# One fused kernel (linear attention, dense units, eight experts): a hand-given order at the passage from the dense units to the experts

## The chip, the core and the metric

The kernel runs on one core of a Trainium2 chip. The metric is the device time in microseconds (us) of one execution, as the median of three runs. The core's engines run side by side, each through its own queue in order: PE (TensorE: matrix products, its weight loads shown as PEld), DVE (VectorE), ACT (ScalarE), POOL (GpSimd) and SP (which here only issues DMAs). They wait for each other through semaphores.

## The reference

Three stages stand one behind the other. A recurrent attention over 768 steps gives 1536 rows (tokens) of 320 numbers. A dense pair of layers follows, and then a top-1 mixture of experts:

```python
def _moe_ref(x, w_in, w_out):                  # 320 -> 2048 -> 320
    h = x @ w_in
    g = np.maximum(0.01 * h, h)
    return (g @ w_out).astype(np.float32)

def _moe2_ref(x, w_gate, w1, w2, capacity):    # 8 experts, capacity 384
    logits = x @ w_gate
    expert_idx = np.argmax(logits, axis=1)
...
    for i in range(N):                          # places in the order of the tokens
        e = expert_idx[i]
        if counts[e] < capacity:
            disp[e, counts[e]] = x[i]
...
    h = np.maximum(np.einsum('ecd,edf->ecf', disp, w1), 0.0)
    y = np.einsum('ecf,efd->ecd', h, w2)
```

The row that a kept token gets back is its gate weight times the row of `y` at its place.

## The kernel before

**Tiles.** The 1536 tokens are twelve tiles of 128, grouped for routing into four blocks: tiles 0 to 3, 4 to 7, 8 to 10 (block 2) and 11 alone (block 3). A value that a product needs in full precision is held as two f16 parts, a high and a low one, so that a product is made of three (or, in the first layers, eight) products of f16.

**Dense units.** `unit(tl, c0, ncc)` makes hidden chunks c0 to c0+ncc-1 (of 16) for the tiles `tl`: eight products per chunk into the PSUM tile `h` (two buffers), then on ACT `t`, on DVE `t` again (the maximum), on ACT the high part `gh`, on POOL the low part `gl`. Its second layer, `close_unit`, comes two units later (LAG is 2): three products per chunk and tile into `px`. When the sixteenth chunk of a tile is in, `route_rows` takes `px` to a row `x2r` (for tile 11 a row that is called `zero`): `split_rows` writes the high part on ACT (L435), the low part on DVE (L436), and copies 64 columns of both on POOL (L439, "the duplicate").

**Routing of a block.** `route_logits` turns the rows (`x2T`): for blocks 0 to 2 by a transposing DMA on SP (L617), for block 3 by six PE transposes into `pt` and one DVE copy (L622, L623). Then come the logits `plg` on PE, the one-hot choice of expert `roh` on DVE, and the products `pp` (L654), which count the tokens ahead of each. `route_scatter` makes of `pp` the place of every token (`slot`) and scatters the rows to the DRAM table `scr`, one indirect DMA on POOL per tile.

**The first expert's input.** Expert e reads its 384 rows by a transposing DMA from `scr` into `xe` (`exp_load`, L822), and `mt` holds the gate weights of all (L827). The first expert does not wait for the last scatters: `exp_first` reads what blocks 0 and 1 put there, and `merge_open` and `merge_close` add the rows of blocks 2 and 3 by products: for each of six parts `pm`, one product with `xe`, three with block 2's rows and the one-hot places `oh`, one with tile 11's. Six casts (three on ACT, L688, three on DVE, L690) bring the sums back.

**Experts.** For each expert, up to three tiles of 128 rows (the second and third under `tc.If`): `hidden` (64 products), `evict` (ACT `hh`, DVE `hl`), `outs` (24 products into `py`), `deliver` (ACT `ye` with `mt`, POOL scatter to the output). Weights come in pieces of 512 hidden columns: a dense `w_in` or `w1` part (`wa`) and a `w_out` or `w2` part (`wc`), each split into high and low parts by `w_in_split` and `w_out_split` on ACT and DVE (L497, L498); pieces 4 and 5 are the first expert's, 6 and 7 the second's. The staging tiles `wa` and `wc` have four buffers each in the expert stage. During an expert, `some(k)` puts a share of the next splits (`bg`) between its steps.

**What sets the order.** A table `ORDER` names the steps in program order: `u11:8+4` is a unit of tile 11, `so6` the `w_out` split of piece 6, `rl2` and `rs2` the two routing steps of block 2, `fl` closes all open units. Up to the end of this table the framework's scheduler is free to put each engine's instructions in another order by its own estimate. From `tc.manual_schedule` on (ahead of the loop over experts) PE, DVE and ACT run in program order; POOL and SP stay the scheduler's.

Of the kernel before, what the change touches and what calls it, by code (L numbers as in the profile page):

```python
# [9 lines left out]
F16 = mybir.dt.float16  # L10
BF16 = mybir.dt.bfloat16
I32 = mybir.dt.int32
# [6 lines left out]
P = 128  # L19
# [28 lines left out]
u2-3:8+2 dec8 x7 og9 u2-3:14+2 tr8 u2-3:0+2 kw7 ld9 st7 cast9 u4-7:7+1 sc8 u4-7:3+1 rl0 kw8 lam9 dec9 tr9 eg8  # L48
# [3 lines left out]
u8-10:3+1 u8-10:8+1 rl1 u8-10:1+1 og11 eg11 st11 u8-10:13+1 u8-10:0+1 dec11 wi5 si5 tr11 sc11 u8-10:7+1 av11  # L52
u8-10:10+1 zf0 wi6 wo4 so4 wo5 si6 out11 x11 sw u8-10:11+1 wl7 wl8 rs1 u8-10:6+1 u8-10:9+1 u8-10:12+1
u8-10:5+1 u8-10:4+1 u8-10:15+1 xe so5 wo6 si7 u11:8+4 so6 u11:4+4 wl9 rl2 so7 rs2 u11:12+4 u11:0+4 fl rl3 rs3
# [3 lines left out]
def program():  # L58
    p = []
    for w in ORDER.split():  # L60
        if w[0] == "u":
            tl, c, n = w[1:].replace("+", ":").split(":")
            tl = [int(x) for x in tl.split("-")]
            p.append(("u", list(range(tl[0], tl[-1] + 1)), int(c), int(n)))
# [10 lines left out]
def tile_mlstm_moe_moe(  # L75
# [358 lines left out]
    def split_rows(r, src, scale, eng):  # L434
# [161 lines left out]
    def route_rows(i, px):  # L596
        bi, o = block_of[i]
        n = len(blocks[bi])
        if bi not in R:
            if n == 1:  # L600
                xr = zero.unsqueeze(1)
            else:
                xr = rows.tile([P, 4, ROW], F32, tag="x2r", name=f"x2r{bi}")
                nc.gpsimd.memset(xr[:, 0:n, 386:], 0.0)
            nc.gpsimd.tensor_scalar(out=xr[:, 0:n, 384:385], in0=tokid[:, i - o:i - o + n].unsqueeze(2), scalar1=1.0,
                                    scalar2=1.0, op0=ALU.mult, op1=ALU.mult)
            R[bi] = xr, a1.tile([P, 4, 6, P], F16, tag="x2T", name=f"x2T{bi}")
        split_rows(R[bi][0][:, o].bitcast(F16), px, 1.0 / (S_IN * S_OUT * S_G), nc.vector)

    def route_logits(bi):  # L610
# [3 lines left out]
        for o in range(n):  # L614
            xo = xr[:, o].bitcast(F16)[:, 0:6 * P]
            if bi < len(blocks) - 1:
                nc.sync.dma_start_transpose(out=x2T[:, o], in_=xo)  # L617
            else:
# [22 lines left out]
        def over_o(x):  # L641
            return x.unsqueeze(1).to_broadcast([P, n, E])
# [6 lines left out]
        nc.vector.tensor_tensor(out=oh, in0=over_o(dec), in1=over_e(u[1]), op=ALU.is_equal)  # L649

# [5 lines left out]
        nc.vector.reciprocal(u[2], inv_all[:, i0:i0 + n])  # L656
        nc.vector.scalar_tensor_tensor(out=t[3], in0=t[1], scalar=1.0 / S_WG, in1=over_e(u[2]), op0=ALU.mult, op1=ALU.mult)
        nc.scalar.activation(t[3], t[3], AF.Exp)
# [33 lines left out]
    def route_scatter(bi):  # L692
# [8 lines left out]
        nc.vector.tensor_tensor(out=base, in0=pp[:, n], in1=base, op=ALU.add)  # L701
# [63 lines left out]
    def unit(tl, c0, ncc):  # L765
# [18 lines left out]
        if len(open_units) > LAG:  # L784
            close_unit()

    def close_all():
        while open_units:
            close_unit()
# [9 lines left out]

    def w_load(n):  # L800
        w_alloc(n)
        w_load_in(n)
        w_load_out(n)
# [3 lines left out]
            "wi": w_load_in, "wo": w_load_out, "si": w_in_split, "so": w_out_split, "u": unit, "fl": close_all,  # L807
            "rl": route_logits, "rs": route_scatter, "zf": zero_fill, "gw": gate_weights}
# [31 lines left out]
    ENG = mybir.EngineType  # L840
    MINE = {ENG.PE, ENG.DVE, ENG.Activation}
# [45 lines left out]
    one = ExitStack()  # L887
    one.enter_context(tc.manual_schedule(engines=MINE))
    for n in range(4, E * NP2):
        pool_of[NP1 + n] = wpb if n % NPC < 3 else pool_of[NP1 + 3] if n % NPC == 3 else wpc  # L890
    for e in range(E):
# [4 lines left out]
        bg = []  # L896
# [82 lines left out]
```

## Time and profile before

| what | value |
|---|---|
| three timed runs | 432.55, 431.89, 428.73 us; median 431.89 |
| the profiled execution's own time | 429.85 us |
| its span from the first to the last instruction | 428.1 us (mean granted TensorE clock 0.965 of full) |
| PE busy | 368.8 us (86%) |
| DVE busy | 296.7 us (69%) |
| ACT busy | 231.3 us (54%) |
| POOL busy | 186.1 us (43%) |

The time is the span and 1.75 us around it. A busy share is a mean over stages: the dense units end near 296 us, the routing of the last tiles lies between 289 and 309 us, and the experts take the rest. Durations and positions in this document are of this one execution.

### The profile page before, as it was taken

Reading aid. Unit: us, or ns where it says so; the run is one execution under the profiler, and the core shown is the slowest. Engines: PE = TensorE matmul, PEld = TensorE weight load, DVE = VectorE, ACT = ScalarE, POOL = GpSimd, SP = SyncE. Lnnn points to the kernel's source line nnn. Section 1 sums busy time; section 2 is a strip of 40 time slices with the busy share of each in tenths; the row PEclk is TensorE's granted clock in tenths of the full one; section 3 lists DMA queues with packets and bytes.
Section 4 is the critical chain, followed back from the end, with each engine's and each line's share of the span. In section 5 each row is a group of like instructions: output and inputs, shape, how many; then the busy total and the mean of one; then the engine's idle time right before and its main releaser. Section 6 shows DMA issues by size and latency. Waiting matters only on the chain. (4 is left out here: it accounts for less than half of the span.)

```text
span 428.1 us, 9161 instructions
## 1 busy us (share of the span) xinstructions
PE 368.8 (86%) x3579; PEld 285.7 (67%) x3579; DVE 296.7 (69%) x507; ACT 231.3 (54%) x445; POOL 186.1 (43%) x214
## 2 busy tenths in 40 slices
PE   0847819889999999999999999797799999789994
PEld 0746708678777876566666676584478888668882
DVE  8959988998978655677563375755558867886121
ACT  3463536637569664646454444861158866875222
POOL 4484792537554564455734364453313221232102
PEclk9999999778989999999999999999689999999998
DMA  9999996319999857179510338999476889933000
GB/s 175 216 321 267 199 239 186 65 26 182 221 206 198 188 122 144 21 200 215 138 54 20 73 137 264 280 283 282 133 124 183 232 261 299 251 83 61 32 18 17
DMA packets 148529, 70.79 MB, mean 165 GB/s; under 512 B 118066, under 2 KB 139092, under 8 KB 148480
## 3 DMA queue, kind: packets, MB, share of 16 engines
q1 hardware_dynamic: 146560, 66.03, 67.8%
q0 software_dynamic: 1920, 4.08, 2.7%
q8 instruction: 34, 0.56, 0.6%
q14 instruction: 15, 0.12, 0.1%
HBM read 43.65 MB, written 13.17 MB: 133 GB/s over the span
## 5 line engine op out<-in xcount | busy, mean ns | idle before, releaser
L585 PEld LDWEIGHTS <-pc 128*128 128x128 f16 x1728 | 118.7, 101 | 30.2 <-issue 9.8
L585 PE MATMUL h<-xT,pc 128*128 128x128 f16 (+3 forms) x768 | 98.4, 282 | 3.5 <-DVE t L780 3.3
L782 POOL TENSOR_TENSOR gl<-t,gh 128x512 f16<-128x512 f32 (+1 forms) x52 | 63.9, 1232 | 48.6 <-ACT gh L781 48.6
L880 POOL DMA_INDIRECT out_dram<-ye,ix x24 | 25.7, 1073 | 83.3 <-ACT ye L879 82.4
L585 PE MATMUL h<-xe,pc 128*128 128x128 f16 x960 | 57.8, 223 | 3.1 <-PEq L921 0.6
L591 PE MATMUL px<-pc,gl 128*128 128x320 f16 x192 | 55.2, 305 | 4.7 <-POOL gl L782 4.6
L589 PE MATMUL px<-pc,gh 128*128 128x320 f16 x192 | 57.7, 304 | 0.3 <-ACT gh L781 0.3
L590 PE MATMUL px<-pc,gh 128*128 128x320 f16 x192 | 57.9, 304 | 0.0
L868 DVE SCALAR_TENSOR_TENSOR hl<-h,hh 128x512 f16<-128x512 f32 x48 | 31.4, 686 | 37.1 <-ACT hh L867 36.0
L780 DVE SCALAR_TENSOR_TENSOR t<-h,t 128x512 f32<-128x512 f32 (+1 forms) x52 | 33.3, 643 | 24.1 <-ACT t L779 24.1
L781 ACT ACTIVATE gh<-t 128x512 f16<-128x512 f32 (+1 forms) x52 | 30.8, 591 | 28.1 <-DVE t L780 28.0
L779 ACT ACTIVATE t<-h 128x512 f32<-128x512 f32 (+1 forms) x52 | 28.6, 553 | 25.3 <-PE h L585 25.0
L867 ACT ACTIVATE hh<-h 128x512 f16<-128x512 f32 x48 | 27.3, 596 | 23.3 <-PE h L585 23.1
L498 DVE SCALAR_TENSOR_TENSOR pc<-wa,pc 128x1024 f16<-128x1024 f32 (+1 forms) x34 | 34.1, 1003 | 6.4 <-ACT pc L497 5.5
L589 PE MATMUL py<-pc,hh 128*128 128x320 f16 x120 | 35.9, 299 | 2.8 <-PEq L924 2.1
L591 PE MATMUL py<-pc,hl 128*128 128x320 f16 x120 | 35.9, 299 | 1.9 <-DVE hl L868 1.4
L590 PE MATMUL py<-pc,hh 128*128 128x320 f16 x120 | 35.9, 299 | 0.0
L497 ACT ACTIVATE pc<-wa 128x1024 f16<-128x1024 f32 (+1 forms) x34 | 27.5, 852 | 9.5 <-DMA wa<-in_moe_w_dram 8.1
L498 DVE SCALAR_TENSOR_TENSOR pc<-wc,pc 128x1280 f16<-128x1280 f32 x18 | 26.8, 1490 | 7.3 <-ACT pc L497 7.0
L591 PEld LDWEIGHTS <-gl 128*128 128x128 f16 x192 | 18.7, 99 | 13.9 <-POOL gl L782 6.8
L497 ACT ACTIVATE pc<-wc 128x1280 f16<-128x1280 f32 x18 | 22.8, 1268 | 5.3 <-DMA wc<-in_moe_w_dram 4.5
L879 ACT ACTIVATE ye<-py,mt 128x320 f32<-128x320 f32 x24 | 12.3, 525 | 23.4 <-PE py L591 12.9
(183 smaller groups left out, 682.4 us busy)
## 6 DMA issues: line engine op xcount, KB each, us to landing
wc<-in_moe_w_dram SPq DMA_DIRECT2D x16, 640.0 KB, 5.9
wa<-in_moe_w_dram SPq DMA_DIRECT2D x16, 512.0 KB, 5.9
raw<-in_moe_w_out_dram SPq DMA_DIRECT2D x4, 1280.0 KB, 8.7
scr<-zero SPq DMA_DIRECT2D x8, 588.0 KB, 4.8
raw<-in_moe_w_in_dram SPq DMA_DIRECT2D x4, 1024.0 KB, 6.2
lb<-lam_d SPq DMA_DIRECT2D x8, 512.0 KB, 4.5
wa<-in_moe_w_dram SPq DMA_DIRECT2D x16, 128.0 KB, 6.0
qkv<-in_k_dram SPq DMA_DIRECT2D x12, 160.0 KB, 4.0
```

Of the source, the lines that this page charges most:

```text
L497: nc.scalar.activation(hi, x, AF.Copy, scale=s)
L498: nc.vector.scalar_tensor_tensor(out=lo, in0=x, scalar=s, in1=hi, op0=ALU.mult, op1=ALU.subtract)
L585: nc.tensor.matmul(ph, lhsT=w, rhs=xT[:, x, 0:ncol], start=(m == 0), stop=(m == len(seq) - 1))
L589: nc.tensor.matmul(py, lhsT=gh, rhs=oh[:, kc, :], start=first, stop=False)
L590: nc.tensor.matmul(py, lhsT=gh, rhs=ol[:, kc, :], start=False, stop=False)
L591: nc.tensor.matmul(py, lhsT=gl, rhs=oh[:, kc, :], start=False, stop=last)
L779: nc.scalar.activation(t, ph, AF.Copy, scale=0.01 * S_G)
L780: nc.vector.scalar_tensor_tensor(out=t, in0=ph, scalar=S_G, in1=t, op0=ALU.mult, op1=ALU.max)
L781: mark[0] = nc.scalar.activation(gh, t, AF.Copy)
L782: nc.gpsimd.tensor_tensor(out=gl, in0=t, in1=gh, op=ALU.subtract)
L867: nc.scalar.activation(hh[:, to[0], to[1]], ph, AF.Relu)
L868: nc.vector.scalar_tensor_tensor(out=hl[:, to[0], to[1]], in0=ph, scalar=0.0, in1=hh[:, to[0], to[1]], op0=ALU.max, op1=ALU.subtract)
```

## The change

Six things are edited. (1) The manual order begins earlier: a step `ms` in the table enters `tc.manual_schedule` after the first unit of tile 11, so the last three units, all routing of blocks 2 and 3 and the merge stand on PE, DVE and ACT as the program writes them. (2) The program's order there is new: the last unit makes its first layer without closing another (`v`), and the three closes (`cl`) stand between the routing steps of block 2. `route_logits` is cut in two (`rl`, `pl`), the second with the products `pp`; the reciprocal and the exponential now stand in the first. (3) Block 2 is turned by PE (`rt0` to `rt2`): 18 transposes and three copies (two DVE, one ACT) in place of three transposing DMAs. (4) In `route_scatter` the one-hot places `oh` and the merge stand ahead of `slot`, the sums and the gate weight. (5) The `w_out` splits of pieces 6 and 7 leave the table and become the first two background items of the first expert. (6) Tile 11's duplicate is made by DVE.

```diff
-u8-10:5+1 u8-10:4+1 u8-10:15+1 xe so5 wo6 si7 u11:8+4 so6 u11:4+4 wl9 rl2 so7 rs2 u11:12+4 u11:0+4 fl rl3 rs3
+u8-10:5+1 u8-10:4+1 u8-10:15+1 xe so5 wo6 si7 u11:8+4 ms u11:4+4 wl9 u11:12+4
+rt0 rt1 rt2 v11:0+4 rl2 cl pl2 cl rs2 cl rl3 pl3 rs3
...
-        nc.gpsimd.tensor_scalar(out=r2[:, :, DM:DM + DC], in0=r2[:, :, 2 * P:2 * P + DC], scalar1=1.0,
+        (dup or nc.gpsimd).tensor_scalar(out=r2[:, :, DM:DM + DC], in0=r2[:, :, 2 * P:2 * P + DC], scalar1=1.0,
...
+    def route_turn(o):
+
+        xr, x2T = R[len(blocks) - 2]
+        pool, tag = (psX, "x") if o == 2 else (psA, "a")
+        pt = pool.tile([P, 6, P], F16, tag=tag, name=f"pt{o}")
+        for c in range(6):
+            nc.tensor.transpose(pt[:, c], xr[:, o].bitcast(F16)[:, c * P:(c + 1) * P], identh)
+        if o == 1:
+            nc.scalar.activation(x2T[:, o], pt, AF.Copy)
+        else:
+            nc.vector.tensor_copy(x2T[:, o], pt)
...
         nc.vector.tensor_tensor(out=t[4], in0=pp[:, 0:n], in1=over_o(base), op=ALU.add)
-        nc.vector.tensor_tensor(out=base, in0=pp[:, n], in1=base, op=ALU.add)
...
-        slot = rows.tile([P, 4], I32, tag=f"slot{bi}", name=f"slot{bi}")
-        nc.vector.tensor_copy(slot[:, 0:n], u[3])
         if bi >= len(blocks) - 2:
...
+        slot = rows.tile([P, 4], I32, tag=f"slot{bi}", name=f"slot{bi}")
+        nc.vector.tensor_copy(slot[:, 0:n], u[3])
+        nc.vector.tensor_tensor(out=base, in0=pp[:, n], in1=base, op=ALU.add)
...
-    one = ExitStack()
-    one.enter_context(tc.manual_schedule(engines=MINE))
...
-        bg = []
+        bg = [lambda: w_out_split(NP1 + 2), lambda: w_out_split(NP1 + 3)] if e == 0 else []
```

**PE, tile 11's routing and the merge.** Before, from the last logits of block 3 (`plg`) to the products with tile 11's places; left out are weight loads and like products:

```order
L630 MATMUL plg_3863<-wgh,x2T_3831 128x8
...
L682 MATMUL pm_3835<-oh_3684,x2r_3600 128x384
L682 MATMUL pm_3840<-oh_3684,x2r_3600 128x384
...
L682 MATMUL pm_3877<-oh_3684,x2r_3600 128x384
...
L654 MATMUL pp_3891<-roh_3884,triu 128x8
...
L686 MATMUL pm_3835<-oh_3905,zero 128x384
```

The same place after:

```order
L701 MATMUL pm_3859<-oh_3817,x2r_3600 128x384
...
L636 MATMUL pt<-identh,zero 128x128
...
L701 MATMUL pm_3872<-oh_3817,x2r_3600 128x384
...
L644 MATMUL plg_3882<-wgh,x2T_3850 128x8
...
L701 MATMUL pm_3891<-oh_3817,x2r_3600 128x384
...
L676 MATMUL pp_3913<-roh_3903,triu 128x8
...
L705 MATMUL pm_3854<-oh_3921,zero 128x384
```

The 18 products of block 2's rows (with the six of `xe`) stood in one piece between the logits and `pp` of block 3; now eight stand ahead of the transposes, eight ahead of the logits and eight between the logits and `pp`.

**DVE, from tile 11's places to the first expert.** `h_...` and `py_...` are PSUM tiles of the experts, cleared here. Before:

```order
L913 MEMSET h_3948 128x512
L703 SCALAR_TENSOR_TENSOR rt_3882<-rt_3882 128x8
L704 TENSOR_TENSOR rt_3882<-rt_3882,roh_3884 128x8
L705 TENSOR_REDUCE ru_3883<-rt_3882 128x1
L707 CAST slot_3903<-ru_3883 128x1
L711 TENSOR_SCALAR oh_3905<-places,ru_3883 128x384
L690 CAST xe_3495<-pm_3840 128x384
L690 CAST xe_3495<-pm_3877 128x384
L913 MEMSET h_3949 128x512
L838 TENSOR_TENSOR filled<-base,lows 1x16
L913 MEMSET py_3951 128x320
L690 CAST xe_3495<-pm_3872 128x384
```

After:

```order
L722 TENSOR_TENSOR rt_3901<-rt_3901,roh_3903 128x8
L723 TENSOR_REDUCE ru_3902<-rt_3901 128x1
L727 TENSOR_SCALAR oh_3921<-places,ru_3902 128x384
L709 CAST xe_3495<-pm_3859 128x384
L709 CAST xe_3495<-pm_3896 128x384
L709 CAST xe_3495<-pm_3891 128x384
L734 CAST slot_3935<-ru_3902 128x1
L735 TENSOR_TENSOR base<-pp_3913,base 128x8
L736 TENSOR_REDUCE ru_3902<-rt_3901 128x1
L737 TENSOR_SCALAR ru_3902<-ru_3902 128x1
L738 RECIPROCAL ru_3902<-ru_3902 128x1
L739 SCALAR_TENSOR_TENSOR zero<-ru_3902 128x1
```

The memsets have left the stretch between `pp` and the last cast; `slot` and the gate weight, on which tile 11's scatter waits, now stand behind the casts.

**ACT, the first expert.** `pc_3252` and `pc_3501` are pieces 6 and 7 by their `wc` part, `pc_3967` and `pc_3984` piece 8, before and after. Before:

```order
L867 ACTIVATE hh_3953<-h_3945 128x4x128
L924 UNCONDITIONAL_BRANCH
L867 ACTIVATE hh_3953<-h_3946 128x4x128
L867 ACTIVATE hh_3953<-h_3947 128x4x128
L867 ACTIVATE hh_3953<-h_3948 128x4x128
L497 ACTIVATE pc_3967<-wa 128x1024
L497 ACTIVATE pc_3967<-wa 64x512
L932 UNCONDITIONAL_BRANCH
L879 ACTIVATE ye_3955<-py_3950,mt 128x320
```

After:

```order
L888 ACTIVATE hh_3972<-h_3965 128x4x128
L943 UNCONDITIONAL_BRANCH
L498 ACTIVATE pc_3252<-wc 128x1280
L888 ACTIVATE hh_3972<-h_3966 128x4x128
L888 ACTIVATE hh_3972<-h_3967 128x4x128
L498 ACTIVATE pc_3501<-wc 128x1280
L900 ACTIVATE ye_3974<-py_3969,mt 128x320
L951 UNCONDITIONAL_BRANCH
L498 ACTIVATE pc_3984<-wa 128x1024
L498 ACTIVATE pc_3984<-wa 64x512
```

Piece 8's split of `wa` has moved behind `ye`, which waits for `mt`, and two splits have come in ahead of it. On SP the transposes of block 2 are gone, and the loads of two later `wc` parts (pieces 10 and 11) have moved from ahead of the first expert to behind its loads of `xe` and `mt`, since the staging buffers are held until pieces 6 and 7 are split.

## Rows read from the trace of the kernel before

**Rows 1.** Timeline, PE, 285 to 319: start, length, what, idle before and its releaser.

```profile
285.86 1.95 PE L585 MATMUL h<-xT,pc 128*128 128x128 f16 x32
...
291.01 0.31 PE L591 MATMUL px<-pc,gl 128*128 128x320 f16 x1 [0.65 <-POOL gl L782]
...
294.06 0.20 PE L630 MATMUL plg<-wgh,x2T 128*128 128x8 f16 x2 [0.39 <-DMA x2T<-x2r]
...
297.50 0.40 PE L622 MATMUL pt<-identh,zero 128*128 128x128 f16 x4
...
298.84 4.76 PE L682 MATMUL pm<-oh,x2r 128*128 128x384 f16 x18
303.44 0.17 PE L654 MATMUL pp<-roh,triu 128*128 128x8 bf16 x1
...
305.68 1.94 PE L686 MATMUL pm<-oh,zero 128*128 128x384 f16 x6 [2.04 <-DVE oh L711]
...
309.11 5.14 PE L585 MATMUL h<-xe,pc 128*128 128x128 f16 x59 [0.55 <-DVE xe L690]
...
318.63 3.73 PE L585 MATMUL h<-xe,pc 128*128 128x128 f16 x64
```

**Rows 2.** Windows: busy PE, PEld, DVE, ACT, POOL; granted clock; DMA share; GB/s.

```profile
272.00:274.00 2.00, 0.10 (x1) 0.09 (x1) 2.00 (x3) 1.72 (x4) 0.00 (x0) 1.00 0.95 200
...
306.00:308.00 2.00, 1.74 (x8) 0.74 (x6) 1.44 (x3) 1.47 (x3) 1.19 (x2) 0.50 0.12 43
```

**Rows 3.** Timeline, DVE, 281 to 306.

```profile
281.91 1.49 DVE L498 SCALAR_TENSOR_TENSOR pc<-wc,pc 128x1280 f16<-128x1280 f32 x1 [1.93 <-ACT pc L497]
...
297.94 0.56 DVE L623 COPY x2T<-pt 128x768 f16<-128x768 f16 x1
...
299.17 0.16 DVE L644 COPY rt<-plg 128x8 f32<-128x8 f32 x1
...
300.15 0.17 DVE L649 TENSOR_TENSOR roh<-dec,ru 128x8 bf16<-128x8 f32 x1
...
304.26 0.48 DVE L913 MEMSET h<- 128x512 f32 x1
...
305.24 0.15 DVE L707 CAST slot<-ru 128x1 int32<-128x1 f32 x1
```

**Rows 4.** Timeline, ACT, 282 to 297.

```profile
282.78 1.08 ACT L435 ACTIVATE x2r<-px 128x320 f16<-128x320 f32 x3
...
296.10 0.44 ACT L435 ACTIVATE zero<-px 128x320 f16<-128x320 f32 x1 [0.47 <-PE px L591]
```

**Rows 5.** Timeline, POOL, 282 to 315.

```profile
282.47 1.95 POOL L782 TENSOR_TENSOR gl<-t,gh 128x512 f16<-128x512 f32 x1 [2.32 <-ACT gh L781]
...
285.14 1.15 POOL L782 TENSOR_TENSOR gl<-t,gh 128x512 f16<-128x512 f32 x1
...
297.15 0.30 POOL L439 TENSOR_SCALAR zero<-zero 128x128 f16<-128x128 f16 x1 [4.72 <-DVE zero L436]
...
306.18 0.97 POOL L723 DMA_INDIRECT scr<-zero,slot  x1 [3.20 <-DVE oh L711]
...
314.94 0.29 POOL L829 TENSOR_SCALAR ix<-mt 128x24 int32<-128x24 f32 x1 [7.56 <-DMA mt<-scr]
```

**Rows 6.** Timeline, SP's DMA issues: start, time in issue.

```profile
308.57 2.28 SPq L822 DMA_TRANSPOSE xe<-scr  x1
310.90 0.57 SPq L827 DMA_DIRECT2D mt<-scr  x1
```

**Rows 7.** Tile xe: time from issue to landing of its DMAs.

```profile
DMA to landing us min/median/max: 4.3/5.2/5.7
```

**Rows 8.** Windows of the expert stage, columns as in rows 2.

```profile
318.50:333.40 14.90, 14.00 (x176) 11.78 (x176) 12.52 (x14) 11.84 (x18) 4.41 (x4) 1.00 0.54 156
333.40:347.60 14.20, 13.85 (x177) 11.87 (x178) 13.24 (x15) 11.91 (x18) 4.18 (x3) 1.00 1.00 273
347.60:361.50 13.90, 13.90 (x217) 12.99 (x215) 8.96 (x11) 7.89 (x12) 2.23 (x2) 1.00 0.90 256
```

More of the change, by code (lines that the diff above doesn't have):

```diff
@@ L60, in program @@
     for w in ORDER.split():
-        if w[0] == "u":
+        if w[0] in "uv":
             tl, c, n = w[1:].replace("+", ":").split(":")
             tl = [int(x) for x in tl.split("-")]
-            p.append(("u", list(range(tl[0], tl[-1] + 1)), int(c), int(n)))
+            p.append((w[0], list(range(tl[0], tl[-1] + 1)), int(c), int(n)))
         else:
@@ L432, in att_out, with split_rows @@
                                 scalar2=float((254 << 23) + (X_EXP << 23)), op0=ALU.mult, op1=ALU.add)
-    def split_rows(r, src, scale, eng):
+    def split_rows(r, src, scale, eng, dup=None):
         mark[0] = nc.scalar.activation(r[:, 0:DM], src, AF.Copy, scale=scale)
@@ L607, in route_rows @@
             R[bi] = xr, a1.tile([P, 4, 6, P], F16, tag="x2T", name=f"x2T{bi}")
-        split_rows(R[bi][0][:, o].bitcast(F16), px, 1.0 / (S_IN * S_OUT * S_G), nc.vector)
+        split_rows(R[bi][0][:, o].bitcast(F16), px, 1.0 / (S_IN * S_OUT * S_G), nc.vector,
+                   nc.vector if i == NTILE - 1 else None)
+    def route_turn(o):
[8 more added lines that the diff above has]
+            nc.vector.tensor_copy(x2T[:, o], pt)
     def route_logits(bi):
@@ L615, in route_logits @@
             xo = xr[:, o].bitcast(F16)[:, 0:6 * P]
-            if bi < len(blocks) - 1:
+            if bi < len(blocks) - 2:
                 nc.sync.dma_start_transpose(out=x2T[:, o], in_=xo)
-            else:
+            elif bi == len(blocks) - 1:
                 merge_open((0, 1))
@@ L649, in route_logits, with route_places @@
         nc.vector.tensor_tensor(out=oh, in0=over_o(dec), in1=over_e(u[1]), op=ALU.is_equal)
+        nc.vector.reciprocal(u[2], inv_all[:, i0:i0 + n])
+        nc.vector.scalar_tensor_tensor(out=t[3], in0=t[1], scalar=1.0 / S_WG, in1=over_e(u[2]), op0=ALU.mult, op1=ALU.mult)
+        nc.scalar.activation(t[3], t[3], AF.Exp)
+        T["rl", bi] = t, u, oh
+    def route_places(bi):
+        n = len(blocks[bi])
+        t, u, oh = T.pop(("rl", bi))
         pp = psA.tile([P, n + 1, E], F32, tag="a", name=f"pp{bi}")
@@ L763, in close_unit, with unit @@
                     route_rows(i, p)
-    def unit(tl, c0, ncc):
+    def unit(tl, c0, ncc, close=True):
         xT, o = xT_of(tl[0])
@@ L783, in unit @@
         open_units.append((tl, xs, c0, ncc, gh, gl))
[L784 to L788, printed above, removed]
+        if close and len(open_units) > LAG:
             close_unit()
@@ L798, in w_room, with manual @@
         nc.gpsimd.iota(T["places"], pattern=[[1, NSLOT]], base=0, channel_multiplier=0, allow_small_or_imprecise_dtypes=True)
+    ENG = mybir.EngineType
+    MINE = {ENG.PE, ENG.DVE, ENG.Activation}
+    one = ExitStack()
+    def manual():
+        one.enter_context(tc.manual_schedule(engines=MINE))
     def w_load(n):
@@ L806, in tile_mlstm_moe_moe @@
             "tr": att_tr, "kw": att_kw, "st": att_state, "sc": att_scores, "av": att_av, "out": att_out, "x": att_x,
-            "wi": w_load_in, "wo": w_load_out, "si": w_in_split, "so": w_out_split, "u": unit, "fl": close_all,
-            "rl": route_logits, "rs": route_scatter, "zf": zero_fill, "gw": gate_weights}
+            "wi": w_load_in, "wo": w_load_out, "si": w_in_split, "so": w_out_split, "u": unit, "v": lambda *a: unit(*a, close=False), "rt": route_turn,
+            "rl": route_logits, "pl": route_places, "cl": close_unit, "ms": manual, "rs": route_scatter, "zf": zero_fill, "gw": gate_weights}
     for f, *a in PROG:
@@ L838, in tile_mlstm_moe_moe @@
     nc.vector.tensor_tensor(out=filled, in0=base[0:1].unsqueeze(2).to_broadcast([1, E, NJ - 1]), in1=lows, op=ALU.is_gt)
-    ENG = mybir.EngineType
-    MINE = {ENG.PE, ENG.DVE, ENG.Activation}
     UC = PC // P
```

7 lines of the change are left out of this document (2 added, 5 removed).

## The prediction

> **What bounds the kernel now.** I read PE's timeline first, since PE is busy 86% of the span, and looked for the stretch in which it is not. That is the passage from the dense units to the experts [rows 1]. Tile 11's last dense product ends just before ACT takes its row at 296.10 [rows 4]; the first expert's hidden products run freely only from 309.11. The 13.0 us between hold little PE work, and the rows say what each step waits for. The one-hot choice `roh` of tile 11 is ready on DVE at 300.15 + 0.17 = 300.32 [rows 3], but its products `pp` start at 303.44, because PE runs in order and 18 merge products stand ahead (298.84, 4.76 us long) [rows 1]. From `pp` to `oh` DVE needs 2.2 us, with a memset in the middle (304.26) [rows 3]; then come the six last merge products and the casts, up to 309.11 [rows 1]. Part of this runs at half the clock: granted 0.50 at 306 to 308, 1.2 GHz in place of 2.4 [rows 2]. Its price shows in like work: 64 hidden products take 3.73 us at 318.63, 59 recorded ones 5.14 us at 309.11 [rows 1]. In the next two windows PE is nearly always busy (14.00 of 14.90, 13.85 of 14.20) [rows 8], so a time won before the second expert reaches the end if ACT, DVE and the weights keep up.
>
> **Up to tile 11's last dense product (gain 0.1).** With block 2 turned by PE two waits for the transposing DMA go (0.39 at 294.06 and one like it of 0.33), POOL's `gl` no longer holds PE for 0.65 at 291.01, and five merge products with `xe` move behind tile 11 [rows 1]. Six like products take 1.94 at half clock (305.68), so one is 0.16 at full clock and the five are 0.8. Added are 18 transposes: four take 0.40 at 297.50, some 0.07 from start to start [rows 1], so 1.2 us. The first of them waits for block 2's rows. ACT takes these at 282.78 now [rows 4]; in the new order they stand behind a `gh` that waits for DVE, which works on a split until 283.4 [rows 3], so they come near 284.6, DVE's halves behind them near 285, and POOL's duplicates once `gl` is out of the way, near 286.2. PE comes to this place at 285.86, where the last unit starts now [rows 1]: I charge 0.35. The copies from PSUM (0.56 each on DVE, as at 297.94 [rows 3]; an estimate of 0.8 on ACT from that) lie under the 32 products of the last unit, 1.95 us [rows 1]. Against these stands a wait of PE for DVE's choice before block 2's `pp`: tile 11's choice takes 1.15 us, from 299.17 to 300.32 [rows 3], with the last unit's `t` ahead of it on DVE and one close of twelve products as cover on PE; between 0 and 1.3 I take 0.5. Removed 2.15, added 2.05: gain 0.1, from -1.5 to 1.
>
> The trace shows POOL's `gl` taking 1.95 us at 282.47, beside DVE's split at 281.91, and 1.15 us at 285.14, beside rows read from PSUM [rows 3, 5]; I took 1.15 for the one ahead of the duplicates. The Trainium skill, "SBUF — State Buffer", section "Who interferes with whom", has the cause: a DVE instruction with two SBUF inputs and a GpSimd one that reads SBUF exclude each other for a whole instruction. It forbids the cheap price only where a split stands next to that `gl`; then the duplicates would come 0.8 later and this term would be -0.7.
>
> **From tile 11's row to `pp` (gain 2.8).** Now 296.10 to 303.44, 7.3 us [rows 1, 4]. After: 0.45 on ACT, 0.5 on DVE, the duplicate on DVE (not in the trace; between DVE's small steps of 0.15 and POOL's 0.30 plus a hand-over [rows 3, 5], I take 0.2), six transposes 0.4 (eight merge products ahead of them lie under ACT and DVE), copy 0.56, logits 0.3, choice 1.15, and about 0.1 at each of three hand-overs. The logits now stand behind eight merge products, 8 x 0.16 = 1.3 us against a copy of 0.6, which adds 0.7; the last eight lie under DVE's choice, if the clock is full. Sum 4.5, gain 2.8. At half clock 16 products cost 1.3 more on either side of the logits; the first 1.3 shows whole, the second is just covered: gain 1.5.
>
> **From `pp` to `oh` (gain 0.5).** 303.44 to 305.68 is 2.24 us [rows 1]. The memset at 304.26 holds 0.4 of it, `base` and `slot` some 0.1 to 0.2 [rows 3]; all three leave.
>
> **Merge and casts (gain 1.2).** 305.68 to 309.11 is 3.43 us [rows 1], at half clock and with two memsets and `filled` between the second and the third cast on DVE. At full clock the products come in 1.0, so the three casts on each engine set the pace at about 0.5 each: 2.2. Gain 1.2; at half clock only the memsets' 0.4.
>
> **First expert's hidden products (gain up to 1.4).** 5.14 against 3.73 for 64 [rows 1] if the clock stays full.
>
> **What caps it.** These add up to 6.0 at full clock and 2.5 at half. But the second expert's `xe` hangs on tile 11's scatter, which now gets `slot` and the gate weight only after the casts. Now `slot` is ready at 305.4, POOL scatters 0.8 later at 306.18, and `xe` is issued 2.4 later at 308.57 [rows 3, 5, 6]; it lands 4.3 to 5.7 after that [rows 7], near 313, long before PE uses it at 318.63 [rows 1]. After, with the passage 4.6 shorter, the casts end near 304.4, six small DVE steps follow (1.25), then the same 0.8 and 2.4: `xe` is issued at 308.85 and lands between 313.1 and 314.5. PE cannot begin the second expert before that, which caps the gain at 4.1 to 5.5, however fast the first expert is. As the landing now is at the short end, I take 5.2.
>
> **Two splits in the first expert (loss 0.3).** Each is 1.49 on DVE, as the one at 281.91 [rows 3], and somewhat less on ACT. Queued behind them are the first expert's second and third evictions, `ye`, piece 8's split and the second expert's evictions; and `ye` waits for `mt`, issued at 310.90 and landed at 314.94 now [rows 5, 6], which comes no earlier. Piece 8's split and the third evictions behind it, some 6 us of ACT and DVE in turn, push the second expert's first `hl` to about 321, where PE, two times 3.73 after 313.5, wants it: I charge 0.3, from 0 to 2. DVE is busy 12.5 of 14.9 and 13.2 of 14.2 us in the next two windows [rows 8], so 3.3 us idle take the two splits' 3.0 only by then. The loads of pieces 10 and 11 (1.28 MB) fall into a window with a DMA share of 0.54 [rows 8].
>
> **Sum.** 0.1 + 2.8 + 0.5 + 1.2 + part of 1.4, held by the cap to 5.2, less 0.3: 4.9 us, 1.1%. Against the profiled execution's 429.85 this gives 424.95. The three timed runs (median 431.89) and this one average 430.8; I take 4.9 off that and forecast **425.9**, with 423.5 to 428.2 as its own range (chance 0.54).
>
> **Rivals.** *The clock falls again* (0.16). For it: PE still idles some 1.5 us between `pp` and the last merge products, and the grant of 0.50 at 306 to 308 came after such a gap (2.04) [rows 1, 2]. Against: after 1.90 idle of 2.00 us at 272 to 274 no lower grant shows [rows 2]. Then the merge and the hidden products run as now: gain 2.5, 428.3. The skill warns of it in "TensorE: Matmul & The Clock Gate", section "What's actually happening": the throttled state is the default, and activity lifts it.
>
> *The given order has nothing to fill its waits with* (0.15). PE stands at `rt0`, at block 2's `pp` and at the second expert's first `hl` for the upper bounds above, 0.8 + 0.8 + 1.7 more than charged: gain 1.6, 429.2. For it: the scheduler filled such gaps with other products, the program order cannot.
>
> *More is won* (0.08): the landing is short and the splits cost nothing: gain 6.0, 424.8 at the least, with a quick run 423.
>
> *Slower* (0.07): the weights become the bound. The two moved `wc` loads wait for splits in the first expert, in one SP queue with the loads of pieces 12 and 13 behind them; 1.28 MB at the 273 GB/s of the saturated window [rows 8] are 4.7 us. If the free 46% of the window before, 6.9 us, cannot take them, the stream of weights ends 4.7 later than now whatever PE has won, and with half-clock products after a wait (1.4) that is 436.9. It decides from the point where a piece lands later than PE asks for it. That the change is not what it says can be left out: the order on PE, DVE and ACT is fixed.
>
> **Numbers.** The range of 8 in 10 is 421.5 to 430.9: the forecast's spread, the clock and waiting cases, and the spread of the runs (3.8 us among three). A change of 1%, 4.3 us, is about what a measurement of this kernel can tell from none, and close to the forecast: 0.40 of its 0.54 and 0.07 of the case of more give 0.47 to faster by over 1%; their rest and the two half-gains 0.46 to within 1%; the slower case 0.07.
>
> **What would show it.** Right: `pp` of tile 11 within 0.3 us of its choice, near 300.5; first hidden products in flow near 304.5; second expert near 313.5, within 1 us of the landing of its `xe`. Wrong: tile 11's last dense product later than 296.5 (the transposes cost more), a grant of 0.50 around 303 to 309 (the clock), a wait on `hl` of over 1 us in the second expert, or on `wa` or `wc` after 335.

## The result and the profile after

The changed kernel takes 426.56 us (median of 20 runs, 423.97 to 430.77) against 432.6 (20 runs, 427.63 to 437.74): a ratio of 0.9884, 95% interval 0.9854 to 0.9914, or 5.0 us of 432. The ratio compares the means (426.6 and 431.6) without the runs that took over 1.5% more than the fastest of their kernel, one of 20 after and five of 20 before, which is why it shows less than the 6.0 between the two medians. A second set (6 runs against 11) gave 0.9854 (0.9807 to 0.9900). The profiled execution took 426.06, 3.8 less than the 429.85 of the one before; its span is 424.3.

PE's timeline of the changed kernel, for [rows 1] (start, length, what, number, idle before and its releaser; PEq is PE's sequencer):

```profile
282.70 1.95 PE L586 MATMUL h<-xT,pc 128*128 128x128 f16 x32
...
286.11 1.17 PE L618 MATMUL pt<-identh,x2r 128*128 128x128 f16 x18
...
292.48 0.18 PE L676 MATMUL pp<-roh,triu 128*128 128x8 bf16 x1 [1.17 <-DVE roh L663]
...
297.27 0.63 PE L636 MATMUL pt<-identh,zero 128*128 128x128 f16 x6
...
300.64 0.18 PE L676 MATMUL pp<-roh,triu 128*128 128x8 bf16 x1
...
302.26 1.14 PE L705 MATMUL pm<-oh,zero 128*128 128x384 f16 x6 [1.42 <-DVE oh L727]
303.93 5.44 PE L586 MATMUL h<-xe,pc 128*128 128x128 f16 x64 [0.53 <-ACT xe L707]
310.21 0.30 PE L590 MATMUL py<-pc,hh 128*128 128x320 f16 x1 [0.84 <-PEq L943]
...
314.88 3.73 PE L586 MATMUL h<-xe,pc 128*128 128x128 f16 x64 [1.26 <-PEq L951]
318.94 3.24 PE L586 MATMUL h<-xe,pc 128*128 128x128 f16 x55 [0.32 <-DVE pc L499]
```

Tile 11's last dense product ends at 296.13, as before. `pp` now starts at 300.64, right behind the choice, where it was 303.44; the six last merge products run at 302.26 in 1.14 us, where 305.68 and 1.94 stood; the first expert flows from 303.93 instead of 309.11. But its 64 products take 5.44, about as much for each as the 59 from 309.11 on took before (5.14; the other five had run at 307.87), and the second expert, which began without a wait for its rows at 318.63, begins at 314.88 behind a wait of 1.26. So 5.4 us are won at 304, and 4.0 are left at the second expert (both counted from the start of the last-but-one dense unit, 282.70 now and 282.44 before). The clock and this wait are the reasons. First the clock; windows as in [rows 2]:

```profile
302.00:304.00 2.00, 1.21 (x8) 0.65 (x8) 1.43 (x4) 1.25 (x3) 0.00 (x0) 1.00 0.00 0
304.00:306.00 2.00, 2.00 (x22) 1.92 (x22) 0.95 (x7) 0.00 (x0) 0.16 (x1) 0.57 0.00 0
306.00:308.00 2.00, 2.00 (x24) 2.00 (x23) 0.79 (x3) 0.60 (x1) 1.02 (x2) 0.57 0.14 51
308.00:310.00 2.00, 1.37 (x25) 1.20 (x22) 1.91 (x5) 0.59 (x2) 0.00 (x0) 1.00 0.18 27
```

A granted 0.57 is a mean of the two levels, 1.2 and 2.4 GHz: in the first of the two windows at 0.57 it fell near 304.3, in the second full speed came back near 307.7.

The chain to the second expert's `xe`, for [rows 5 to 7]: POOL's scatter, SP's issues, the landing, and POOL's first use of `mt`.

```profile
284.39 1.16 POOL L801 TENSOR_TENSOR gl<-t,gh 128x512 f16<-128x512 f32 x1 [0.33 <-ACT gh L800]
285.51 0.83 POOL L440 TENSOR_SCALAR x2r<-x2r 128x128 f16<-128x128 f16 x3
...
305.84 0.97 POOL L742 DMA_INDIRECT scr<-zero,slot  x1 [5.83 <-DVE zero L739]
...
315.46 0.29 POOL L852 TENSOR_SCALAR ix<-mt 128x24 int32<-128x24 f32 x1 [8.45 <-DMA mt<-scr]
```

```profile
308.23 2.39 SPq L845 DMA_TRANSPOSE xe<-scr  x1
310.66 0.58 SPq L850 DMA_DIRECT2D mt<-scr  x1
```

```profile
DMA to landing us min/median/max: 6.1/6.1/6.1
```

`xe` is issued at 308.23 and lands 6.1 later, at 314.33. PE's first weight load of the second expert starts only at 314.85, though, and it loads `pc`, not `xe`. What it waits for shows in the rows of the test that stands between the two experts (the second tile of the first expert, under `tc.If`), in PE's own sequencer; of the changed kernel, and of the kernel before:

```profile
L951 PEldq COMPARE_BRANCH  x2: 63/1869/3675, 311.0 to 323.4; - x2
```

```profile
L932 PEldq COMPARE_BRANCH  x2: 63/142/222, 315.9 to 327.1; - x2
```

The columns are the number of them, the shortest, middle and longest in ns, and the first and last start. The first of the two lasted 3.675 us from 311.0 on, to 314.7, 0.4 behind the landing; before, 0.22 from 315.9 on.

### The profile page after: what moved, and what is told of

It is laid out like the page before. It is cut to its first block, busy times and chain, and to the rows that moved or that the text cites. A ratio compares the mean times of both kernels' runs of the same rounds, so it can differ in the third digit from the quotient of the medians.

```text
span 424.3 us, 9192 instructions
## 1 busy us (share of the span) xinstructions
PE 365.2 (86%) x3597; PEld 285.5 (67%) x3597; DVE 297.3 (70%) x510; ACT 231.9 (55%) x446; POOL 183.7 (43%) x213
## 5 line engine op out<-in xcount | busy, mean ns | idle before, releaser
L801 POOL TENSOR_TENSOR gl<-t,gh 128x512 f16<-128x512 f32 (+1 forms) x52 | 62.3, 1198 | 55.6 <-ACT gh L800 55.2
L592 PE MATMUL px<-pc,gl 128*128 128x320 f16 x192 | 56.2, 308 | 4.6 <-POOL gl L801 4.6
L591 PEld LDWEIGHTS <-gh 128*128 128x128 f16 x192 | 19.2, 100 | 8.7
```

The costliest lines, as they stand in the source:

```text
L591: nc.tensor.matmul(py, lhsT=gh, rhs=ol[:, kc, :], start=False, stop=False)
L592: nc.tensor.matmul(py, lhsT=gl, rhs=oh[:, kc, :], start=False, stop=last)
L801: nc.gpsimd.tensor_tensor(out=gl, in0=t, in1=gh, op=ALU.subtract)
```

## The experiments

Two quantities are compared besides the times. The **passage** runs from the start of the last-but-one dense unit's products to the second expert's first product; the **rest** from there to the end of the span. The start of the passage differs by up to 5 us between executions in which nothing ahead of it was changed, so a span alone says little of an edit behind it. "First expert" is the time of its 64 hidden products; where 59 stands beside it, five had run ahead of the last casts.

| kernel | passage starts | first expert | passage | rest | ratio of timed runs (95%) |
|---|---|---|---|---|---|
| before | 282.44 | 5.14 (59) | 36.19 | 109.47 | 1 |
| before, second profile | 284.02 | 5.54 (59) | 36.53 | 109.65 | |
| changed | 282.70 | 5.44 | 32.18 | 109.42 | 0.9884 (0.9854 to 0.9914) |
| changed, second profile | 285.20 | 3.85 | 31.46 | 111.34 | 0.9854 (0.9807 to 0.9900) |
| e1 order by the scheduler | 283.16 | 5.24 (59) | 35.66 | 109.48 | 0.9960 (0.9924 to 0.9995) |
| e2 merge products first | 280.69 | 3.85 | 35.21 | 111.40 | 1.0000 (0.9955 to 1.0045) |
| e3 block 2 by DMA | 285.58 | 3.85 | 37.07 | 110.45 | 1.0086 (1.0041 to 1.0130) |
| e4 scatter first | 284.53 | 3.90 | 30.08 | 109.49 | 0.9883 (0.9832 to 0.9934) |
| e5 fill | 283.37 | 3.85 | 31.86 | 111.87 | 0.9876 (0.9839 to 0.9913) |
| e6 splits back | 281.52 | 3.85 | 39.93 | 110.25 | 1.0062 (1.0030 to 1.0094) |
| e7 close as cover | 283.80 | 5.36 | 31.41 | 112.79 | 0.9846 (0.9803 to 0.9889) |
| e8 cover and scatter | 281.70 | 5.39 | 30.91 | 109.79 | 0.9841 (0.9803 to 0.9878) |
| e11 no branch | 284.05 | 3.90 | 27.69 | 109.76 | 0.9768 (0.9722 to 0.9814) |
| e12 all that helped | 282.82 | 3.90 | 29.07 | 111.01 | 0.9745 (0.9704 to 0.9787) |

**e1: the order by the scheduler.** The new steps stay; the given order begins with the experts again.

```diff
-... so5 wo6 si7 u11:8+4 ms u11:4+4 wl9 u11:12+4
+... so5 wo6 si7 u11:8+4 u11:4+4 wl9 u11:12+4
...
+    manual()
     for e in range(E):
```

> The changed program with all its new steps, but the order on PE, DVE and ACT from tile 11's last dense units on is left to the scheduler, as before the change (the given order begins only with the experts). Theory A (the given order carries most of the gain): the scheduler again puts merge products ahead of tile 11's logits and memsets between `pp` and the casts; `pp` of tile 11 comes 1 to 2 us later than the 300.6 of the changed kernel, the first hidden products flow near 307 instead of 303.9, the second expert starts near 317.5 instead of 314.9, and the time is 428.5 to 430. Theory B (the new steps carry it, whoever orders them): within 1 us of the changed kernel's 426.6, second expert by 315.5.

The passage is 35.66, 3.5 longer than in the changed kernel and 0.5 shorter than before; the time 429.03. By the same rows as above the scheduler wins 0.5 up to tile 11's last product (12.91 after the start of the passage, against 13.43) by filling the wait at block 2's `pp`, and loses 1.5 up to `pp`, 0.9 from there to the last merge products and 2.3 to the first expert, with memsets between the casts and the merge products at half clock:

```profile
302.03 0.19 PE L676 MATMUL pp<-roh,triu 128*128 128x8 bf16 x1 [1.25 <-DVE roh L663]
...
304.54 2.08 PE L705 MATMUL pm<-oh,zero 128*128 128x384 f16 x6 [2.29 <-DVE slot L734]
...
308.46 5.24 PE L586 MATMUL h<-xe,pc 128*128 128x128 f16 x59 [0.25 <-DVE xe L709]
...
318.82 3.34 PE L586 MATMUL h<-xe,pc 128*128 128x128 f16 x57 [0.94 <-PEq L952]
```

Theory A holds: the order carries 3.5 of the 4.0 us in the passage. But the second expert waits 0.94 here, with its `xe` there since 312.0 (4.3 after its issue), for "PEq": the wait ahead of it isn't the landing's alone.

**e2: the merge products first.**

```diff
-                merge_open((0, 1))
                 pt = psA.tile([P, 6, P], F16, tag="a", name="pt")
...
-                merge_open((2, 4))
...
-            merge_open((5, 3))
+            merge_open((0, 1, 2, 4, 5, 3))
```

> All 24 merge products with `xe` and block 2's rows stand between tile 11's logits and its `pp`, instead of around the transposes and the logits; nothing else is changed. Theory A (the place of `pp` in PE's order is the largest term): the logits come 0.5 earlier, then 24 products of 0.163 = 3.9 us hold `pp`, which comes near 302.6 at full clock, or near 304.8 if the products run at half clock after PE's wait; everything behind, the scatter and the second expert's `xe` with it, comes 2.0 to 4.2 later: 428.6 to 430.8. Theory B (the second expert's start hangs on something else, a transfer or the splits): at most 0.5 later, 426.6 to 427.1.

The passage grows by 3.0, to 35.21, and the whole gain is gone (ratio 1.0000). From the last dense product to `pp` it takes 8.2 where the changed kernel takes 4.5. PE stood three times ahead of the products (0.53, 0.55 and 0.65 us), the clock fell (0.50 at 298 to 300), and some twelve of them ran at half speed, so the loss is one of place and of clock together. The first expert ran at full clock here; beside the changed kernel's second profile, where it did too, the passage is 3.75 longer. What stands ahead of `pp` in PE's queue is the largest term, as theory A has it. The rest is 2.0 longer as well: see e5.

**e3: block 2 turned by DMA again.**

```diff
-        pool, tag = (psX, "x") if o == 2 else (psA, "a")
-        pt = pool.tile([P, 6, P], F16, tag=tag, name=f"pt{o}")
...
-            nc.vector.tensor_copy(x2T[:, o], pt)
+        nc.sync.dma_start_transpose(out=x2T[:, o], in_=xr[:, o].bitcast(F16)[:, 0:6 * P])
```

> Block 2 is turned by three transposing DMAs on SP again, at the place in the program where TensorE now turns it; the rest of the change stays. Theory A (in the given order nothing covers the DMA): the rows are whole near 286.3, the first transpose lands 6.4 to 7.1 later, the last near 295; PE stands at block 2's logits from 288.0 on for 5 to 7 us with only what is ahead of them done, and the time is 431 to 434, about that of the kernel before. Theory B (the transfers were nearly hidden before, 0.7 us of waits, and are so again): 426.8 to 427.6.

```profile
296.36 0.22 PE L637 MATMUL plg<-wgh,x2T 128*128 128x8 f16 x2 [5.42 <-DMA x2T<-x2r]
```

PE stands 5.42 us for the first transfer; the time is 433.91, theory A. Before, the DMA cost waits of 0.39 and 0.33, with closes and merge products put ahead of the logits by the scheduler; in this order nothing stands there. The transposes on PE make the order possible; that they win anything by themselves isn't shown.

**e4: the scatter first.**

```diff
...
         nc.vector.tensor_copy(slot[:, 0:n], u[3])
-        nc.vector.tensor_tensor(out=base, in0=pp[:, n], in1=base, op=ALU.add)
...
                                        op0=ALU.mult, op1=ALU.mult)
+        if bi == len(blocks) - 1:
+            merge_close(xr[:, 0].bitcast(F16), oh0[:, 0])
+        nc.vector.tensor_tensor(out=base, in0=pp[:, n], in1=base, op=ALU.add)
```

> On DVE tile 11's `slot` and gate weight (five small steps) stand between `oh` and the casts instead of behind the casts; `base` alone stays behind. Theory A (the second expert's start hangs on the landing of its `xe`, which hangs on tile 11's scatter): the casts and the first hidden products come 0.3 later (304.2), the scatter about 1.8 earlier (near 304.0), `xe` is issued near 306.4 instead of 308.2 and lands near 313; the wait of 1.26 at the second expert falls below 0.5, and it starts 0.3 to 0.8 earlier than 314.88: 425.8 to 426.3. Theory B (the second expert waits for something else, the branch or the hidden layer's banks): it starts 0.3 later, 426.9.

The scatter comes 20.9 after the start of the passage instead of 23.1, the first expert no later (21.16 and 21.23), the passage falls by 2.1 to 30.08. That is more than expected: the first expert's products ran at full clock here (3.90, not 5.44), behind the same waits of 1.42 and 0.53. So 1.5 of it may be the clock's, and the timed ratio (0.9883) shows nothing beyond the changed kernel's. Beside the changed kernel's second profile (e9), with the first expert at full clock as well, the passage is 1.4 shorter (30.08 and 31.46). The wait ahead of the second expert is still 0.82, not below 0.5, and it is again the weight load that waits:

```profile
313.49 0.30 PE L592 MATMUL py<-pc,hl 128*128 128x320 f16 x1
...
314.58 0.41 PEld L586 LDWEIGHTS <-pc 128*128 128x128 f16 x7 [1.13 <-issue]
314.61 0.49 PE L586 MATMUL h<-xe,pc 128*128 128x128 f16 x6 [0.82 <-PEq L951]
```

**e5: the waits filled.** Eight products behind `pp` and three behind the last merge products keep PE busy.

```diff
         T["rr", bi] = t, u, oh, pp
+        if bi == len(blocks) - 1:
+            T["warm"] = psA.tile([P, NSLOT], F32, tag="a", name="warm")
+            for _ in range(8):
+                nc.tensor.matmul(T["warm"], lhsT=identh, rhs=X[0][:, 0], start=True, stop=True)
...
+        for _ in range(3):
+            nc.tensor.matmul(T["warm"], lhsT=xo[:, 0:P], rhs=oh, start=True, stop=True)
```

> Eight products into an unused PSUM tile are added on PE between tile 11's `pp` and the six last merge products, three more behind those; they fill the waits of 1.42 and 0.53 us, and their results are not used. The clock should then stay at 1.00 where the changed kernel shows 0.57 (304 to 308), and the 64 hidden products of the first expert take 3.8 to 3.9 instead of 5.44. The passage is measured from the start of the last-but-one dense unit to the second expert's first product: 32.2 us in the changed kernel, 36.2 in the kernel before. Theory A (the landing of the second expert's `xe` holds its start): the wait ahead of the second expert grows from 1.26 to about 2.8 and the passage stays at 32.2 (32.0 to 32.6): 426.4 to 427.0. Theory B (the first expert's products at half clock hold it): the passage falls to 30.7 or so, 425.0.

The clock stayed at 1.00 and the first expert took 3.85, yet the time did not move (0.9876): theory B is out. Nor is it as theory A told it: the passage is 31.86, with a wait of 0.67 for the landing. PE gave most back earlier, 1.44 at the test ahead of the first expert's `outs` and 0.57 for `hl`. Both hang on tile 11's scatter too. The test needs `filled`, for which DVE stands 2.01 us, since POOL makes `lows` only behind that scatter; then PE's sequencer loads `filled`, from 308.4 on, in 1.33 us, and the test can start at 309.9:

```profile
308.24 0.16 DVE L867 TENSOR_TENSOR filled<-base,lows 1x16 int32<-1x16 f32 x1 [2.01 <-POOL lows L864]
```

```profile
L942 PEldq TENSOR_LOAD <-filled x1: 1326/1326/1326, 308.4 to 308.4; - x1
```

On DVE the memsets and the first expert's `hl` stand behind `filled`. In the changed kernel's first profile the slow products end at 309.37 and hide this; in e4, at full clock but with the earlier scatter, the wait ahead of `outs` is 0.78 and the one for `hl` is gone.

The rest grew to 111.87. There `mt`, issued at 311.69, was used only 6.50 later (4.80 in the changed kernel), ACT stood in front of `ye`, and piece 8's split and the next evictions behind it came late:

```profile
318.19 0.53 ACT L906 ACTIVATE ye<-py,mt 128x320 f32<-128x320 f32 x1 [5.32 <-DMA mt<-scr]
318.62 1.56 ACT L498 ACTIVATE pc<-wa 128x1024 f16<-128x1024 f32 x2
```

```profile
322.41 1.95 PE L586 MATMUL h<-xe,pc 128*128 128x128 f16 x32 [1.18 <-DVE hl L895]
...
325.02 0.31 PE L592 MATMUL py<-pc,hl 128*128 128x320 f16 x1 [0.39 <-DVE hl L895]
```

This is the prediction's chain behind the two moved splits, at 1.6 us instead of 0.3; the changed kernel's second profile shows it too (waits of 1.12 and 0.38, `mt` used 6.44 after its issue, rest 111.34). It goes with the late `mt`, not with the fast first expert alone: in e4, as fast, `mt` was used 4.8 after its issue, and no such wait shows.

**e6: the two splits back in the table.**

```diff
-... u11:8+4 ms u11:4+4 wl9 u11:12+4
+... u11:8+4 ms so6 u11:4+4 wl9 so7 u11:12+4
...
-        bg = [lambda: w_out_split(NP1 + 2), lambda: w_out_split(NP1 + 3)] if e == 0 else []
+        bg = []
```

> The splits `so6` and `so7` stand in the table again, ahead of tile 11's next-to-last units and ahead of `wl9`'s neighbour, as in the old table, but inside the given order; the first expert has none. Theory A (ACT and DVE have no room there): each split pushes the evictions behind it by 1.3 to 1.5, PE waits for block 2's rows and for the last units' `gl`, and the passage grows from 32.2 by 1.5 to 3, to 33.7 to 35.2: 428 to 429.6. Theory B (they lie in ACT's and DVE's idle time): passage within 0.3 of 32.2. By both, the stretch from the second expert to the end stays within 0.3 of the 109.4 of the changed kernel.

The passage is 7.7 longer, far more than 1.5 to 3, and not for the splits' own time. ACT stands in front of piece 6's part, which has not landed, and with it everything behind it in ACT's queue:

```profile
285.22 1.27 ACT L498 ACTIVATE pc<-wc 128x1280 f16<-128x1280 f32 x1 [5.35 <-DMA wc<-in_moe_w_dram]
```

In the kernel before the scheduler had put this split at 287.14, behind the rows of block 2. In the first expert it cost nothing in the profiles in which `mt` was in time.

**e7: a close as cover.**

```diff
-rt0 rt1 rt2 v11:0+4 rl2 cl pl2 cl rs2 cl rl3 pl3 rs3
+rt0 rt1 rt2 v11:0+4 rl2 cl cl pl2 rs2 cl rl3 pl3 rs3
```

> One of the closes of tile 11's units moves from behind block 2's `pp` and scatter to ahead of that `pp`, so that PE has 24 instead of 12 dense products to do while DVE chooses; nothing else is changed. Theory A (the wait of 1.17 at block 2's `pp` is on the path, as the prediction charged 0.5 for it): the wait goes, the last close now has `oh` of block 2 nearly ready behind it, and tile 11's row comes 0.7 to 1.1 earlier from the start of the last-but-one unit (13.4 now); the scatter and the second expert come as much earlier: passage 31.1 to 31.5, 425.5 to 426. Theory B (the path up to tile 11's row runs through DVE or POOL, not PE): row and passage within 0.2 of now.

The wait of 1.17 is gone, tile 11's row comes 1.3 earlier (12.09 instead of 13.43), the passage is 0.8 shorter (31.41), as theory A has it; 0.38 of the time won went into a wait for DVE at the transposes. The profiled execution lost it again in the rest: 1.35 at another test, and a grant of 0.50 at 374 to 376 behind a wait of 1.51 for `hl` in the fifth expert (1.4 to 1.5 in every kernel here but e11, 0.8). The timed ratio, 0.9846, can't be told from the changed kernel's.

**e8: both.** The diffs of e4 and e7 together.

> The moved close and the earlier `slot` and gate weight of tile 11 together. With the scatter first alone the passage was 30.1 us, at full clock in the first expert, against 32.2 in the changed kernel, and the second expert still waited 0.82 for its `xe`. Theory A (row, scatter and landing are one chain): the gains add, passage 29.0 to 29.5 at full clock and up to 30.5 if the first expert's products run at half clock; 109.4 behind it; 424 to 425.5. Theory B (another wait takes over, the splits and evictions of the first expert or `mt`): passage not below 29.9, or the stretch behind it longer than 110.

`xe` is issued 22.8 after the start of the passage (25.5 in the changed kernel), and lands at 308.8, 3.8 before PE uses it, but the passage is 30.91, theory B by its number: with the first expert at half clock (5.39) and the test of 3.1 us, the second expert starts where these let it. Here the landing holds nothing.

**e9, e10: both kernels once more.**

> The changed kernel once more, unchanged. The passage is measured as before, from the start of the last-but-one dense unit to the second expert's first product (32.2 in the first profile), then the stretch to the end (109.4). Theory A (the spread of the runs comes from the stages ahead of the passage and from chance in the first expert): the passage is 31.5 to 33.5, the stretch behind it 109.4 to 112, the start of the last-but-one unit anywhere from 280.5 to 285; ratio to the kernel before again 0.985 to 0.992. Theory B (the first profile was an odd one): the passage within 1 us of the 36.2 of the kernel before.

> The kernel before once more, unchanged, for a second profile. Theory A (the first profile of it is typical): passage 35.5 to 37, stretch behind it 109.2 to 110; the profiles then give a gain of 3.5 to 4.5 us in the passage, and the rest of the 5.0 us that the timed runs show is chance. Theory B (the first profile of it was a lucky one): the passage is 37 or longer, and the gain is nearer to 6.

Theory A in both (e9's passage of 31.46 and its start at 285.20 lie just outside the ranges given). Two profiles of each give passage and rest together 145.66 and 146.18 before, 141.60 and 142.80 after: a gain of 2.9 to 4.6, where the timed runs show 5.0 (3.7 to 6.3).

**e11: no branch.** e8, and for the first expert alone:

```diff
...
-        with if_block(e, 1):
-            hidden(e, 1)
+        if e > 0:
+            with if_block(e, 1):
+                hidden(e, 1)
...
+            if e > 0:
+                with if_block(e, 1):
+                    outs(e, 1)
```

> The moved close and the earlier scatter (both as in the run that had them together), and of the first expert only its first block: the tests and the products of its second and third blocks, which these inputs leave empty, are left out, so PE meets no branch before the second expert. Theory A (the second expert starts late because PE's sequencer is held in a branch: the test for the second block took 3.1 us there, 3.7 in the changed kernel, 0.2 in the kernel before, and the first weight load behind it waited 0.98): that weight load follows within 0.2 us of the last product, and the products start at once or wait for `xe` alone; passage 30.9 falls to 29.8 to 30.5. Theory B (the landing of `xe` holds the start, and the sequencer's row only marks it): the same start, passage 30.7 to 31.1.

PE's weight loads, then its products, at the passage from the first to the second expert:

```profile
311.47 0.10 PEld L592 LDWEIGHTS <-hl 128*128 128x128 f16 x1
311.60 1.07 PEld L586 LDWEIGHTS <-pc 128*128 128x128 f16 x17
```

```profile
308.48 0.30 PE L590 MATMUL py<-pc,hh 128*128 128x320 f16 x1 [0.24 <-issue]
...
311.60 0.30 PE L592 MATMUL py<-pc,hl 128*128 128x320 f16 x1
311.74 0.94 PE L586 MATMUL h<-xe,pc 128*128 128x128 f16 x14
```

No weight load waits, `xe` landed at 310.9 (4.4 after its issue), and the passage is 27.69: 3.2 shorter than e8's, of which the full clock is 1.5 and the tests, here and ahead of `outs` (0.24 where e8 has 0.82), the rest. Theory A holds, since the weight loads follow at once; the passage lies 2.1 below its range, 1.5 of that by the clock, which the range had at half. The ratio is 0.9768.

**e12: all that helped.** The diffs of e5 and e8, and `some(2)` of the first expert ahead of `outs` and `deliver`.

> Everything that helped, together: the moved close, the earlier scatter, the eleven products of no use that keep PE's clock up, and piece 8's split of `wa` ahead of the first expert's `ye`, as in the kernel before, since with the fill alone ACT stood 5.3 us at `ye` and the second expert waited 1.2 and 0.4 for `hl`. Theory A (these were the limits, in this order): first expert at full clock, passage 29 to 30, no wait on `hl` above 0.5 in the second expert, stretch behind it 109.4 to 110.2; 421.5 to 424 or a ratio of 0.975 to 0.982. Theory B (branch or landing hold the second expert whatever is done ahead): passage not below 30.5.

The passage is 29.07 and no wait for `hl` shows in the second expert, theory A. But `mt` was used 4.9 after its issue, so the run doesn't test what the moved split of piece 8 is worth. Beside e11, at full clock in both, the passage shows 1.4 for the tests. The rest of this execution is 111.01, above theory A's range, since the clock fell behind the `hl` wait of the fifth expert (0.50 at 368 to 370). The time is 422.18, the ratio 0.9745 (0.9704 to 0.9787), below the interval of the changed kernel on the same chip (0.9807 to 0.9900): the fastest kernel of the study, though its interval overlaps e11's (0.9722 to 0.9814).

## Why the prediction was right, and where it was off

The forecast of 425.9 was 0.7 below the 426.56 that came, its gain of 4.9 us beside 5.0. The order on PE, the mechanism that it named, is shown by e1 and e2. That the numbers agree so well is in part luck: it started from 430.8, where the 20 runs before have a median of 432.6, and a gain of 6.0 between the medians made up for most of this; and inside the passage a term too small (the merge) and one that did not come (the first expert's clock) offset each other. Term by term, by the first profile:

- *Up to tile 11's last dense product*, gain 0.1: measured 0.2 (13.62 to 13.43 from the start of the passage). Its parts were off both ways: no wait for block 2's rows (0.35 charged; the duplicates end at 286.34, the first transpose starts at 286.11), 1.17 at block 2's `pp` (0.5 charged, 1.3 the bound). POOL's `gl` ahead of the duplicates took 1.16, and the one beside DVE's split 1.94, so the cheap price was the right one. The trace agrees here with the rule of the Trainium skill, "SBUF — State Buffer", section "Who interferes with whom".
- *From the row to `pp`*, gain 2.8: 7.38 to 4.51, 2.9. e2 takes it away, and its passage is 3.0 longer. The reason is only half of the one given, the 18 products ahead of `pp`. They took 4.76, 0.26 each, since the clock had already fallen in the kernel before, behind waits of 0.32, 0.24 and 0.65 and not only after the gap of 2.04 that the prediction names:

```profile
300.00:302.00 2.00, 2.00 (x8) 0.99 (x7) 1.31 (x7) 0.21 (x1) 1.39 (x2) 0.50 1.10 280
```

At the 0.163 of full clock the 18 would have taken 2.9. Of the 3.1 that `pp` stood behind its choice some 1.5 were thus the products' place and 1.6 the clock (an estimate from these rows). In the changed kernel PE has no such waits there, and the grant stays at 1.00 from 298 to 304.

- *From `pp` to `oh`*, 0.5: 2.24 to 1.62, 0.6. *Merge and casts*, 1.2: 3.43 to 1.67, 1.8; all at full clock.
- *First expert's hidden products*, up to 1.4: nothing in the first profile, all of it in the second. (The 59 before were not records of 64 with five lost: those five had run at 307.87.) The clock that the rival *the clock falls again* feared did fall, and one of the prediction's own signs of being wrong showed with it (0.57 at 304 to 308), but behind the merge products and in a place where a faster PE gains nothing while the scatter stays where it is (e5).
- *The cap*, 5.2: this is the mis-sized term. 4.0 was left at the second expert in the first profile, 4.9 in the second by the mean of before. It was reasoned from the landing of `xe` alone, at the short end of 4.3 to 5.7; the landing took 6.1, and a second limit, the test in PE's sequencer (3.7 us where the kernel before showed 0.22), lay 0.4 behind it. In the second profile the landing itself held PE, by 0.78, and the test did not. A third limit the prediction put at nothing: `filled`, behind the same scatter, held PE by 1.45 ahead of the first expert's `outs` there. e4 moves the scatter, and so the landing and `filled` together; which of them its gain comes from was not separated. e11 takes the tests away. Each shortens the passage at equal clock, by 1.4 beside e9 and by 1.4 beside e12.
- *Two splits in the first expert*, loss 0.3: 0 in the first profile (the wait ahead of the second tile is 0.32, as before), 1.6 in e5 and 1.5 in the second profile, where `mt` came late. The bound of 2 was right.
- *Given order can't fill its waits*: only the wait of 1.17 came, at 0.7 more than charged. *Slower*: DMA's share of 314.3 to 329.2 rose to 1.02, from 0.54 in the like window before [rows 8], and yet PE waits for no `wa` or `wc` behind 335 (before, once for 0.43). The two loads are 1.31 MB (2 x 128 x 1280 numbers of 4 bytes), not 1.28, which changes little.

What stays open: two profiles of each kernel give 2.9 to 4.6 us where the timed runs give 5.0 and more; whether the stages ahead of the passage gain something as well, or two profiles are too few, was not tried. Nor is it shown why the test takes 0.2 us in some executions and 3.7 in others, or why `mt` was used 5.7 to 6.6 after its issue in five profiles (e2, e3, e5, e6, e9) and 4.0 to 4.9 in the others. What kept the clock up in the changed order was not tested by itself either.

## What to carry to other kernels

In a queue that runs in order, look first at what stands ahead of the one small instruction that everybody waits for: here 18 products ahead of two were worth 3 us, about half of it because they ran at half clock. An order given by hand has to bring cover for every long wait: a transfer and a split that the scheduler had walked around cost 5.42 and 5.35 us of standing in it (e3, e6). And at the next hand-over look for more than one limit (here the landing, the test, and the value that the test reads): what moving the first saves, the next keeps until it is moved as well.

## What the runs showed of the hardware

A conditional block that isn't taken is not always cheap. Here PE's sequencer reaches the test some 2.6 us before the last product ahead of it ends (311.0 and 313.63 in the changed kernel), so a test of 0.2 us or even of 2.0 (e5, e9) costs next to nothing, while 3.1 to 3.7 (changed, e1, e4, e7, e8, e12) goes with waits of PE of 0.7 to 1.3. The Trainium skill, "Advanced Engine Details and Errata", section "Control Flow Timing", gives about 108 ns for a compare-and-branch; rows here give 63 to 3675 ns for the same instruction, so the measurement decides. What makes a test long was not separated. The value that the test reads has its price as well: loading the 16 numbers of `filled` took PE's sequencer 1.3 us (e5, e9).

The clock falls in some executions only. Behind the same waits of 1.42 (1.51 in e8) and 0.53 us it fell to 0.57 or less, by windows of 2 us, in the first expert of the changed kernel, e7 and e8, and stayed at 1.00 in e3, e4, e6, e9 and e11.
